# Turning three quarters of x and the query weight in the DMA, and moving the sums of Z, in a two-branch linear attention kernel

## The chip, the cores and the metric

The kernel runs on one core of one Trainium2 chip. The metric is the device time of one execution in microseconds; the kernel before takes 341.06 us (median of 3 runs, 340.96 to 342.13). A core has five engines that run side by side and wait for each other through semaphores: PE (TensorE, matmuls and transposes by matmul), DVE (VectorE), ACT (ScalarE), POOL (GpSimd) and SP (SyncE, which here only issues DMAs). Each engine carries out its instructions in the order of the program.

## The reference

Two attention branches read the same x (2048 tokens of 640 numbers, 32 heads of 20) and are mixed by a gate. Branch A makes features from softmaxes over the 20 numbers of a head, in both signs, and is linear in the keys:

```python
x = A_x
g = _sigmoid((x * gate_w).sum(-1, keepdims=True))
a = _A_ref(x, A_wqkv, A_w_phi, A_wo)
b = _B_ref(x, B_wq, B_wk, B_wv, B_wo, B_beta)
return g * a + (1 - g) * b
...
phi_q = jnp.concatenate([_softmax(pq, axis=-1), _softmax(-pq, axis=-1)], axis=-1)
phi_k = jnp.concatenate([_softmax(pk, axis=-1), _softmax(-pk, axis=-1)], axis=-1)
kv = jnp.einsum('bhsf,bhsd->bhfd', phi_k, v)
z = jnp.einsum('bhsf->bhf', phi_k)
num = jnp.einsum('bhqf,bhfd->bhqd', phi_q, kv)
den = jnp.einsum('bhqf,bhf->bhq', phi_q, z)[..., None] + 1e-06
o = num / den
```

Here z is the sum of the key features over all 2048 tokens. Branch B is causal softmax attention in four segments of 512 tokens with a memory carried from segment to segment; the change doesn't touch it.

## The kernel before

The order of every engine's instructions is that of the program text (manual schedules). The work falls into stages.

**Loading and folding (lines 95 to 308).** SP issues the loads of half the key weight, of x in eight pieces of 256 tokens (`emit_xload`, line 99, tile x_nat, six buffers), of the gate vector and of the value weight WvA. The key weight is turned on PE (`emit_foldT`: five transposes into PSUM and one copy to WkT), and multiplied with w_phi (`emit_foldM`) into WkA. `emit_xT(sc)` turns 128 tokens of x: five PE transposes (xtp, line 190) and one ACT copy into xT (line 192). Chunks 0 to 3 are turned among the fold products.

**The key loop (lines 312 to 322), 16 chunks of 128 tokens.** In step sc PE first turns x for chunk sc+4; then `emit_a1(sc)` makes ten matmuls to pk and ten to pv (line 214). A chunk is not 128 consecutive tokens: chunk sc = 4g + r holds every fourth token, starting with r, of the 512 tokens of quarter g (xTk, line 206). ACT takes two exponentials (Ek, line 218) and copies pv to vA (line 220); DVE sums over the 20 numbers of a head (ksum, line 222) and inverts (krec, line 225); POOL multiplies (EkSn, line 226). `emit_zmove(sc)` issues two DMAs from SP (line 234), one for each sign: they fold EkSn's 128 token rows into 16 partitions of Z with 8 rows each. In steps 9 to 13 PE also turns one fifth of the query weight (wnat_q, loaded in step 2) into WkT; after the loop `emit_foldM` multiplies it to WqA (line 325).

**Sums over tokens (lines 378 to 387).** `emit_kv(j, sgn, scs)` sums key features times values over the chunks on PE (kv_ps, line 368), in two PSUM tiles, one for each sign; DVE takes each block out with a mask (kvn, line 373). Blocks 0 and 3 come first (chunks 0 to 13, then 14 and 15), then 1, 2 and 4. `emit_zadd(ts)` (line 239) adds rows t of Z to row 0, one DVE instruction for each of the 31 rows: rows 1 to 5 behind block 1, 6 to 13 behind block 2, 14 to 31 behind block 4. SP then issues the loads of branch B's weights and the two output weights (lines 396 and 401).

**Query features (lines 479 to 494).** Ten steps (qb, j) of `emit_pq`: ten matmuls (pq, line 265) and two ACT exponentials (Eq, line 270). After step (0, 4) DVE finishes the gate (`emit_gS`). After step (1, 0) come `emit_z` (five PE transposes of Z's row 0, zt), `emit_zz` (33 small DVE instructions, lines 249 to 252, and two products to kvd, line 254) and POOL memsets over Z (`open_stages`). After step (1, 3) PE makes the denominators of chunks 0 to 3 (`emit_den`, line 410, 48 small matmuls of kvd), and DVE and POOL turn them into factors (`den_chain`).

**The loop over the 16 query chunks (line 528) and branch B** follow. The loop opens with the numerators of chunk 0 (line 527, tiles num0 and num1) and the denominators of chunks 4 and 5, whose PSUM tiles take over the memory of the tiles before. The transposing DMAs that the kernel already has are here: lines 520 (128 x 1024 numbers) and 556 (128 x 640), from SBUF to SBUF.

Of the kernel before, what the change touches and what calls it, by code (L numbers as in the profile page):

```python
# [7 lines left out]
ACT = mybir.ActivationFunctionType  # L8
ALU = mybir.AluOpType
BF16 = mybir.dt.bfloat16  # L10
# [5 lines left out]
def kernel(  # L16
# [15 lines left out]
    nc = tc.nc  # L32
    P = 128
    S = 2048
# [22 lines left out]
    back = const.tile([P, 4, 4, 8, 4], BF16, name="back")  # L57
# [14 lines left out]
    wq_stack = ExitStack()  # L72
    wq_hold = wq_stack.enter_context(tc.tile_pool(name="wq_hold", bufs=1))
    x_stack = ExitStack()
    xload = x_stack.enter_context(tc.tile_pool(name="xload", bufs=6))
    aps_stack = ExitStack()
    aps = aps_stack.enter_context(tc.tile_pool(name="aps", bufs=4, space=bass.MemoryType.PSUM))

    wnat_k = wq_hold.tile([P, KC, D], BF16, name="wnat_k", tag="wnat")
# [7 lines left out]
    def wsrc(lo):  # L87
        return A_wqkv[:, lo:lo + D].rearrange("(c p) n -> p c n", p=P)
# [19 lines left out]
    nc.sync.dma_start(out=gw5, in_=gate_w.rearrange("(c p) -> c p", p=P))  # L108
    for bk in range(2):
        nc.sync.dma_start(out=WvA[:, :, bk, 0:320], in_=wsrc(2 * D)[:, :, bk * 320:(bk + 1) * 320])  # L110
    for n in range(4):
        emit_xload()
    nc.sync.dma_start(out=beta_b, in_=B_beta.partition_broadcast(P))

    nc.gpsimd.memset(ident_b, 0.0)
# [32 lines left out]
                                fill=val, base=-row, channel_multiplier=1)  # L148


    nc.gpsimd.memset(back, 0.0)
# [4 lines left out]
    for u in range(4):  # L156
        nc.gpsimd.tensor_copy(out=back[:, u, :, :, u], in_=r32.rearrange("p (b t) -> p b t", t=8))

    def emit_Wphi(j):
        h0, h1 = TH[j]  # L160
        nc.vector.tensor_tensor(out=Wphi[:, j, 0:h1 - h0, :],
# [4 lines left out]
    def w2tile(name):  # L166
        return aps.tile([P, 2, 512], F32, name=name, tag="w2")
# [19 lines left out]
    def emit_xT(sc):  # L187
        tp = aps.tile([P, KC, P], BF16, name="xtp", tag="w2")
        for c in range(KC):
            nc.tensor.transpose(out=tp[:, c, :], in_=x_nat[sc // 2][:, sc % 2, c * P:(c + 1) * P],  # L190
                                identity=ident_b)
        nc.scalar.copy(out=xT[:, :, sc * P:(sc + 1) * P], in_=tp)
# [4 lines left out]
    a1w = kv_stack.enter_context(tc.tile_pool(name="a1work", bufs=3, side="right"))  # L197
    kvpool = kv_stack.enter_context(tc.tile_pool(name="kvpool", bufs=1, side="right"))
    EkSn = kvpool.tile([P, NCH, 2, D], BF16, name="EkSn")
    vA = kvpool.tile([P, NCH, 2, 321], BF16, name="vA")  # L200
    zt = zpool.tile([P, KC, P], BF16, name="zt")
    zz = zpool.tile([P, KC, 2, 2], BF16, name="zz")
# [2 lines left out]

    xTk = xT.rearrange("p c (g m r) -> p c g r m", g=4, r=4)

    def emit_a1(sc):
        pk, pv = w2tile("pk"), w2tile("pv")
        for ps, W, n in ((pk, WkA, 320), (pv, WvA, 321)):  # L210
            for bk in range(2):
                for c in range(KC):
                    rhs = WvA[:, c, bk, :] if W is WvA else WkA[:, c, bk * 320:(bk + 1) * 320]
                    nc.tensor.matmul(ps[:, bk, 0:n], lhsT=xTk[:, c, sc // 4, sc % 4], rhs=rhs,  # L214
                                     start=(c == 0), stop=(c == KC - 1))
# [10 lines left out]
        nc.gpsimd.tensor_tensor(  # L226
            out=EkSn[:, sc].rearrange("p s (h f) -> p (s h) f", f=DH),
            in0=Ek.rearrange("p s (h f) -> p (s h) f", f=DH),
            in1=krec[:, :, None].to_broadcast([P, 2 * H, DH]), op=ALU.mult)

    def emit_zmove(sc):
        g, r = divmod(sc, 4)
        for sgn in range(2):
            nc.sync.dma_start(out=Z[64 * sgn + 16 * g:64 * sgn + 16 * g + 16, r:32:4],
                              in_=EkSn[:, sc, sgn, :])

    def emit_zadd(ts):
        for t in ts:
            nc.vector.tensor_tensor(out=Z[:, 0, :], in0=Z[:, 0, :], in1=Z[:, t, :], op=ALU.add)
# [5 lines left out]
        nc.vector.tensor_copy(out=zt, in_=zt_ps)  # L245

    def emit_zz():
        ztv = zt.rearrange("p j (s h w) -> p j s h w", s=2, h=2)
        nc.vector.tensor_copy(out=zz, in_=ztv[:, :, :, :, 0])
        for w in range(1, 32):  # L250
            nc.vector.tensor_tensor(out=zz, in0=zz, in1=ztv[:, :, :, :, w], op=ALU.add)  # L251
        nc.vector.tensor_tensor(out=zcol, in0=zz[:, :, :, 0], in1=zz[:, :, :, 1], op=ALU.add)
        for sgn in range(2):
            nc.vector.tensor_tensor(out=kvd[:, sgn, :, :, 0], in0=wmw,
                                    in1=zcol[:, :, sgn:sgn + 1].to_broadcast([P, KC, HW]), op=ALU.mult)

    HB = 1024
    Eqs = {}
    def emit_pq(qb, j):
        Eq = Eq0[:, j] if qb == 0 else a3e.tile([P, 2, HB], BF16, name="Eq")  # L260
        pq = w2tile("pq")
        for half in range(2):
            for c in range(KC):
                t0 = qb * HB + half * 512
                nc.tensor.matmul(pq[:, half, :], lhsT=WqA[:, c, j * P:(j + 1) * P],  # L265
                                 rhs=xT[:, c, t0:t0 + 512],
                                 start=(c == 0), stop=(c == KC - 1))
        pqf = pq.rearrange("p b n -> p (b n)")
        for sgn in range(2):
            nc.scalar.activation(out=Eq[:, sgn, :], in_=pqf, func=ACT.Exp, scale=1.0 - 2.0 * sgn)  # L270
        Eqs[qb, j] = Eq

    def emit_beta():
        eb = const.tile([P, H], F32, name="eb")
# [31 lines left out]
    nc.tensor.transpose(out=gw_ps, in_=gw5, identity=ident_b[0:KC, 0:KC])  # L306
    nc.vector.tensor_copy(out=WvA[:, :, :, 320:321],
                          in_=gw_ps[:, :, None, None].to_broadcast([P, KC, 2, 1]))
    for n in range(2):
        emit_xload()  # L310
    wnat_q = wq_hold.tile([P, KC, D], BF16, name="wnat_q", tag="wnat")
    for sc in range(NCH):
        if sc + 4 < NCH:
            emit_xT(sc + 4)
        emit_a1(sc)
        emit_zmove(sc)
        if sc == 2:
            nc.sync.dma_start(out=wnat_q, in_=wsrc(0))
        if sc == 7:
            omgh_b, CM = emit_beta()  # L320
        if 9 <= sc < 14:
            emit_foldT(wnat_q, WkT, sc - 9, nc.scalar.copy if sc % 2 else nc.vector.tensor_copy)
    x_stack.close()
    for n in range(KC):
        emit_foldM(WkT, WqA, n)
# [12 lines left out]
    def emit_gate():  # L338
        gt_ps = aps.tile([P, NCH], F32, name="gt_ps", tag="w2")
        for u in range(4):  # L340
            nc.tensor.matmul(gt_ps, lhsT=back[:, u].rearrange("p b t v -> p (b t v)"),
                             rhs=xg[:, u].rearrange("p g a -> p (g a)"), start=(u == 0), stop=(u == 3))
        nc.scalar.activation(out=eg, in_=gt_ps, func=ACT.Exp, scale=-1.0)

    def emit_gS():
# [8 lines left out]
    def emit_kv(j, sgn, scs):  # L354
# [16 lines left out]
        if scs[-1] == NCH - 1:  # L371
# [3 lines left out]
                in0=kv_tiles[sgn][:, bk, off:off + n].rearrange("p (h d) -> p h d", d=DH),  # L375
                in1=wmw[:, j, h0 - g0:h1 - g0, None].to_broadcast([P, h1 - h0, DH]), op=ALU.mult)

    for scs in (range(14), range(14, NCH)):
        for j in (0, 3):
            for sgn in range(2):  # L380
                emit_kv(j, sgn, scs)
    for j, ts in ((1, range(1, 6)), (2, range(6, 14)), (4, range(14, 32))):
        for sgn in range(2):
            emit_kv(j, sgn, range(NCH))
        if j == 1:
            emit_gate()
        emit_zadd(ts)
# [582 lines left out]
```

## Time and profile before

| | us |
|---|---|
| Median of the runs | 341.06 |
| Profiled execution, its own time | 340.92 |
| Its span, first to last instruction | 339.2 |
| PE busy | 317.5 |
| ACT busy | 259.6 |
| DVE busy | 224.8 |
| POOL busy | 209.2 |

The stages in the span: loading and folding to 12.4 us, the key loop to 60.6, fold of the query weight to 62.7, sums over tokens to 75.1, query features to 101.6, the query loop to about 142, branch B to the end. The granted TensorE clock is 0.995 on the mean. A chain line gives start, duration, engine and tile or line; a timeline line gives start, duration, engine, line, operation, tiles, shape, count and, in brackets, how long the engine had been idle and who released it.

### The profile page before, as it was taken

The numbers are of one execution on the slowest core, as the hardware profiler recorded it, in microseconds if no ns is written. First come the engines' busy times: TensorE is split into PE (matmuls) and PEld (weight loads), VectorE is DVE, ScalarE is ACT, GpSimd is POOL, SyncE is SP. The second block draws the span as 40 slices with busy tenths as digits, with TensorE's granted clock in tenths as the row PEclk, the third lists the DMA queues.
The fourth block names the chain that finished last, engine by engine and source line by source line (L and its number), as shares of the span: only waits on it lengthen the run. The fifth ranks groups of instructions, "written<-read, shape, count | busy, mean of one in ns | idle before, by whom it ended". The sixth has DMA issues, their size and how long they took to land.

```text
span 339.2 us, 9735 instructions
## 1 busy us (share of the span) xinstructions
PE 317.5 (94%) x4021; PEld 219.2 (65%) x4021; DVE 224.8 (66%) x448; ACT 259.6 (77%) x331; POOL 209.2 (62%) x301
## 2 busy tenths in 40 slices
PE   6899999989978999988999999999999999999994
PEld 6788888874436877745665556556666656665662
DVE  3466887479877889726877686767666665453452
ACT  4888887508845455689999999999889889889842
POOL 8177678500406878864766666767867777666540
PEclk9999999999979999999999999999999999999999
DMA  8839969896003688754633255363564663421222
GB/s 232 277 70 180 121 96 118 123 294 208 0 2 24 124 117 122 119 107 81 95 64 57 41 101 95 58 108 64 92 83 87 123 88 73 87 60 51 45 72 77
DMA packets 83381, 34.21 MB, mean 101 GB/s; under 512 B 69258, under 2 KB 83338, under 8 KB 83338
## 3 DMA queue, kind: packets, MB, share of 16 engines
q1 hardware_dynamic: 82906, 33.11, 52.5%
q8 instruction: 31, 0.51, 0.7%
q10 hardware_dynamic: 432, 0.49, 0.6%
q14 instruction: 12, 0.10, 0.1%
HBM read 9.21 MB, written 2.62 MB: 35 GB/s over the span
## 4 chain that ended last, share of the span: by engine, by line
PE 61%; ACT 17%; DVE 10%; DMA 6%; issue 4%; POOL 1%; SPq 0%; ACTq 0%; DVEq 0%
ACT PT L625 15%; PE st_ps L621 10%; PE proj L755 9%; PE nda L677 7%; PE pk L214 6%; PE pv L214 6%; PE proj L808 6%; PE pq L265 5%; PE proj L506 3%; DVE tt L454 3%; DMA x_nat<-in_A_x_dram 2%; PE num L410 2%; DVE zz L251 2%; DVE rr L432 2%; DMA Z<-EkSn 1%
## 5 line engine op out<-in xcount | busy, mean ns | idle before, releaser
L625 ACT ACTIVATE PT<-st_ps 128x1024 bf16<-128x1024 f32 x160 | 154.4, 1025 | 15.9 <-PE st_ps L621 13.2
L632 POOL TENSOR_SCALAR_AFFINE_SELECT PT<-PT 128x512 bf16<-128x512 bf16 (+1 forms) x130 | 86.9, 687 | 48.0 <-ACT PT L625 47.9
L226 POOL TENSOR_TENSOR EkSn<-Ek,krec 128x1280 bf16<-128x1280 bf16 x16 | 37.6, 2358 | 17.9 <-DVE krec L225 16.2
L677 PEld LDWEIGHTS <-PT 128*128 128x128 bf16 x1280 | 39.8, 96 | 11.6 <-issue 8.4
L677 PE MATMUL nda<-vB,PT 128*128 128x21 bf16 x1280 | 42.8, 173 | 1.2 <-DVE mtmp L720 0.8
L214 PEld LDWEIGHTS <-xTf 128*128 128x128 bf16 x320 | 35.3, 113 | 6.8
L808 PEld LDWEIGHTS <-xTf 128*128 128x128 bf16 x320 | 28.0, 97 | 17.3 <-issue 8.0
L814 DVE CAST Z<-proj 128x320 bf16<-128x320 f32 x48 | 22.8, 486 | 22.6 <-PE proj L808 22.1
L222 DVE TENSOR_REDUCE ksum<-Ek 128x64 f32<-128x1280 bf16 x16 | 23.6, 1478 | 12.7 <-ACT Ek L218 12.7
L270 ACT ACTIVATE Eq<-pq 128x1024 bf16<-128x1024 f32 x20 | 19.4, 1021 | 14.2 <-PE pq L265 14.2
L454 DVE TENSOR_TENSOR tt<-num,rr 128x640 f32<-128x640 f32 x32 | 25.2, 812 | 6.2 <-PE num L410 4.3
L621 PE MATMUL st_ps<-Z 32*128 32x512 bf16 (+3 forms) x256 | 24.9, 299 | 4.1 <-ACT PT L625 2.1
L545 POOL TENSOR_TENSOR oA<-tt 128x640 bf16<-128x640 f32 x16 | 24.6, 1543 | 5.1 <-DVE tt L454 4.4
L755 PE MATMUL proj<-WkA,oTA 128*128 128x320 bf16 x160 | 27.3, 299 | 0.0
L218 ACT ACTIVATE Ek<-pk 128x640 bf16<-128x640 f32 x32 | 20.8, 701 | 7.5 <-PE pk L214 5.0
L410 PEld LDWEIGHTS <-Eq 128*128 128x128 bf16 x384 | 20.3, 97 | 9.4 <-issue 6.7
L621 PE MATMUL st_ps<-Eq 32*128 32x384 bf16 (+3 forms) x256 | 24.8, 299 | 1.4 <-ACT PT L625 0.8
L717 POOL TENSOR_TENSOR oB<-td 128x320 bf16<-128x320 f32 x23 | 19.8, 861 | 8.9 <-DVE td L714 5.8
L214 PE MATMUL pv<-WvA,xTf 128*128 128x321 bf16 x160 | 24.6, 300 | 0.0
L214 PE MATMUL pk<-WkA,xTf 128*128 128x320 bf16 x160 | 24.3, 299 | 0.0
L265 PE MATMUL pq<-xTf,WqA 128*128 128x512 bf16 x100 | 23.1, 392 | 0.0
L755 PE MATMUL proj<-WvA,oT 128*128 128x320 bf16 x120 | 22.6, 300 | 0.0
(142 smaller groups left out, 544.4 us busy)
## 6 DMA issues: line engine op xcount, KB each, us to landing
Z<-EkSn SPq DMA_DIRECT2D x32, 160.0 KB, 4.9
x_nat<-in_A_x_dram SPq DMA_DIRECT2D x8, 320.0 KB, 6.5
out_dram<-orow SPq DMA_DIRECT2D x10, 160.0 KB, 1.9
WvA<-in_A_wqkv_dram SPq DMA_DIRECT2D x2, 400.0 KB, 6.5
wnat_q<-in_A_wqkv_dram SPq DMA_DIRECT2D x1, 800.0 KB
WkB<-in_B_wk_dram SPq DMA_DIRECT2D x1, 800.0 KB, 7.2
WqB<-in_B_wq_dram SPq DMA_DIRECT2D x1, 800.0 KB, 9.0
WvB<-in_B_wv_dram SPq DMA_DIRECT2D x1, 800.0 KB, 10.6
```

Source lines behind the costliest of these rows:

```text
L214: nc.tensor.matmul(ps[:, bk, 0:n], lhsT=xTk[:, c, sc // 4, sc % 4], rhs=rhs, start=(c == 0), stop=(c == KC - 1))
L226: nc.gpsimd.tensor_tensor(out=EkSn[:, sc].rearrange("p s (h f) -> p (s h) f", f=DH), in0=Ek.rearrange("p s (h f) -> p (s h) f", f=DH), in1 ...
L265: nc.tensor.matmul(pq[:, half, :], lhsT=WqA[:, c, j * P:(j + 1) * P], rhs=xT[:, c, t0:t0 + 512], start=(c == 0), stop=(c == KC - 1))
L410: nc.tensor.matmul(ps(bk, lo, hi), lhsT=Eqs[qb, j][:, sgn, qc * P:(qc + 1) * P], rhs=kvx[:, sgn, j, lo - h0:hi - h0, :].rearrange("p h e - ...
L454: nc.vector.tensor_tensor(out=tt[:, sgn].rearrange("p (b h) d -> p b h d", b=2), in0=ps, in1=csb, op=ALU.mult)
L545: nc.gpsimd.tensor_tensor(out=oA.rearrange("p (h d) -> p h d", d=DH), in0=tt[:, 0], in1=tt[:, 1], op=ALU.add)
L621: nc.tensor.matmul(ps[:, i - i0, o:o + L - c * P], lhsT=kT[32 * i:32 * i + 32, c * P:(c + 1) * P], rhs=qT[32 * i:32 * i + 32, c * P:L], st ...
L625: nc.scalar.activation(out=PT[:, i0:i0 + 2], in_=ps, func=ACT.Exp, scale=SCALE_B)
L632: nc.gpsimd.affine_select(out=v, in_=v, pattern=[[0, n_i], [1, P]], compare_op=ALU.is_ge, fill=0.0, base=0, channel_multiplier=-1)
L677: nc.tensor.matmul(nd[:, j, i], lhsT=block(st, c)[:, i, (j - c) * P:(j - c + 1) * P], rhs=vB[:, c, 4 * st.g + i, :], start=(c == 0), stop= ...
L755: nc.tensor.matmul(ps, lhsT=oT[:, k % KC], rhs=W[:, k % KC, hs], start=(k == 0), stop=(k == n - 1))
L808: nc.tensor.matmul(ps, lhsT=xT[:, k, sc * P:(sc + 1) * P], rhs=W[:, k, half * 320:(half + 1) * 320], start=(k == 0), stop=(k == KC - 1))
```

## The change

Four things change, in what the instructions do and where they stand.

1. Only the first quarter of x is still loaded as x_nat and turned on PE. The other three quarters go into xT by three transposing DMAs from HBM, 512 x 640 numbers each (`emit_xturn`): two are issued by SP behind the loads of WvA, the third behind the Z moves of step 1. The query weight goes into WkT by one transposing DMA, issued behind the Z moves of step 5.
2. The chunks of the last quarter hold runs of 8 consecutive tokens, 16 runs 32 tokens apart. ACT gathers them from xT into a tile xP with four copies in steps 8 to 11 (`emit_xrun`). The Z moves write partitions 4 apart, and the last quarter's chunk r fills rows 8r to 8r+7 of Z; `emit_zz` reads the columns in the matching order. The gate takes its last four columns with a second set of matrices, back_run.
3. The 31 additions of Z stand elsewhere: rows 1 to 3 behind step 14 of the key loop, 4 to 9 before blocks 0 and 3, 10 to 15 behind these, 16 to 21 behind block 1, 22 and 23 behind block 2, 24 to 31 behind block 4.
4. `emit_gS`, `emit_z`, `emit_zz` and `open_stages` stand before query step (0, 4), and the first denominators behind step (1, 2).

```diff
-    xload = x_stack.enter_context(tc.tile_pool(name="xload", bufs=6))
+    xload = x_stack.enter_context(tc.tile_pool(name="xload", bufs=2))
...
+    xP = wq_hold.tile([P, KC, S // 4], BF16, name="xP")
...
-    for n in range(4):
-        emit_xload()
+
+    def emit_xturn(g):
+        nc.sync.dma_start_transpose(out=xT[:, :, 512 * g:512 * g + 512], in_=x2[512 * g:512 * g + 512, :])
+
+    def emit_xrun(r):
+        nc.scalar.copy(out=xP[:, :, r * P:(r + 1) * P].rearrange("p c (s u) -> p c s u", u=8),
+                       in_=xT[:, :, 1536:2048].rearrange("p c (s r u) -> p c s r u", r=4, u=8)[:, :, :, r])
+
+    emit_xturn(1)
+    emit_xturn(2)
...
+    def key_tokens(c, sc):
+
+        g, r = divmod(sc, 4)
+        return xTk[:, c, g, r] if g < 3 else xP[:, c, r * P:(r + 1) * P]
...
-            nc.sync.dma_start(out=Z[64 * sgn + 16 * g:64 * sgn + 16 * g + 16, r:32:4],
+            nc.sync.dma_start(out=Z[64 * sgn + g:64 * sgn + 64:4, r:32:4] if g < 3 else
+                              Z[64 * sgn + g:64 * sgn + 64:4, 8 * r:8 * r + 8],
                               in_=EkSn[:, sc, sgn, :])
...
-    for n in range(2):
-        emit_xload()
-    wnat_q = wq_hold.tile([P, KC, D], BF16, name="wnat_q", tag="wnat")
     for sc in range(NCH):
-        if sc + 4 < NCH:
-            emit_xT(sc + 4)
         emit_a1(sc)
         emit_zmove(sc)
-        if sc == 2:
-            nc.sync.dma_start(out=wnat_q, in_=wsrc(0))
+        if sc == 1:
+            emit_xturn(3)
+        if 8 <= sc < 12:
+            emit_xrun(sc - 8)
         if sc == 7:
             omgh_b, CM = emit_beta()
-        if 9 <= sc < 14:
-            emit_foldT(wnat_q, WkT, sc - 9, nc.scalar.copy if sc % 2 else nc.vector.tensor_copy)
+        if sc == 5:
+            nc.sync.dma_start_transpose(out=WkT, in_=A_wqkv[:, 0:D])
+        if sc == 14:
+            emit_zadd(range(1, 4))
...
+    emit_zadd(range(4, 10))
     for scs in (range(14), range(14, NCH)):
         for j in (0, 3):
             for sgn in range(2):
                 emit_kv(j, sgn, scs)
-    for j, ts in ((1, range(1, 6)), (2, range(6, 14)), (4, range(14, 32))):
+    emit_zadd(range(10, 16))
+    for j, ts in ((1, range(16, 22)), (2, range(22, 24)), (4, range(24, 32))):
         for sgn in range(2):
             emit_kv(j, sgn, range(NCH))
...
         for j in range(KC):
-            emit_pq(qb, j)
             if (qb, j) == (0, KC - 1):
                 emit_gS()
-            if (qb, j) == (1, 0):
                 emit_z()
                 emit_zz()
                 open_stages()
-            if (qb, j) == (1, 3):
+            emit_pq(qb, j)
+            if (qb, j) == (1, 2):
```

More of the change, by code (lines that the diff above doesn't have):

```diff
@@ L56 @@
     bd01 = const.tile([P, 4], F32, name="bd01")
-    back = const.tile([P, 4, 4, 8, 4], BF16, name="back")
     EPS_HI = 1.0 / 2 ** 20 + 3.0 / 2 ** 26
@@ L74 @@
     x_stack = ExitStack()
-    xload = x_stack.enter_context(tc.tile_pool(name="xload", bufs=6))
+    xload = x_stack.enter_context(tc.tile_pool(name="xload", bufs=2))
     aps_stack = ExitStack()
     aps = aps_stack.enter_context(tc.tile_pool(name="aps", bufs=4, space=bass.MemoryType.PSUM))
-    wnat_k = wq_hold.tile([P, KC, D], BF16, name="wnat_k", tag="wnat")
+    wnat_k = wq_hold.tile([P, KC, D], BF16, name="wnat_k")
+    xP = wq_hold.tile([P, KC, S // 4], BF16, name="xP")
     Wc = wq_hold.tile([P, KC, DH], BF16, name="Wc")
@@ L148 @@
                                 fill=val, base=-row, channel_multiplier=1)
-    nc.gpsimd.memset(back, 0.0)
     r32 = const.tile([P, 32], BF16, name="r32")
@@ L155 @@
         nc.gpsimd.tensor_tensor(out=r32, in0=r32, in1=ident_b[:, 32 * n:32 * n + 32], op=ALU.add)
-    for u in range(4):
-        nc.gpsimd.tensor_copy(out=back[:, u, :, :, u], in_=r32.rearrange("p (b t) -> p b t", t=8))
     def emit_Wphi(j):
@@ L199 @@
     EkSn = kvpool.tile([P, NCH, 2, D], BF16, name="EkSn")
+    back = kvpool.tile([P, 4, 4, 8, 4], BF16, name="back")
+    back_run = kvpool.tile([P, 4, 4, 4, 8], BF16, name="back_run")
+    nc.gpsimd.memset(back, 0.0)
+    for u in range(4):
+        nc.gpsimd.tensor_copy(out=back[:, u, :, :, u], in_=r32.rearrange("p (b t) -> p b t", t=8))
+    nc.gpsimd.memset(back_run, 0.0)
+    for u in range(4):
+        nc.gpsimd.tensor_copy(out=back_run[:, u, :, u, :], in_=r32.rearrange("p (b t) -> p b t", t=8))
     vA = kvpool.tile([P, NCH, 2, 321], BF16, name="vA")
@@ L213, in emit_a1 @@
                     rhs = WvA[:, c, bk, :] if W is WvA else WkA[:, c, bk * 320:(bk + 1) * 320]
-                    nc.tensor.matmul(ps[:, bk, 0:n], lhsT=xTk[:, c, sc // 4, sc % 4], rhs=rhs,
+                    nc.tensor.matmul(ps[:, bk, 0:n], lhsT=key_tokens(c, sc), rhs=rhs,
                                      start=(c == 0), stop=(c == KC - 1))
@@ L247, in emit_zz @@
     def emit_zz():
-        ztv = zt.rearrange("p j (s h w) -> p j s h w", s=2, h=2)
-        nc.vector.tensor_copy(out=zz, in_=ztv[:, :, :, :, 0])
+        ztv = zt.rearrange("p j (s a h b) -> p j s h b a", s=2, h=2, b=2)
+        nc.vector.tensor_copy(out=zz, in_=ztv[:, :, :, :, 0, 0])
         for w in range(1, 32):
-            nc.vector.tensor_tensor(out=zz, in0=zz, in1=ztv[:, :, :, :, w], op=ALU.add)
+            nc.vector.tensor_tensor(out=zz, in0=zz, in1=ztv[:, :, :, :, w // 16, w % 16], op=ALU.add)
         nc.vector.tensor_tensor(out=zcol, in0=zz[:, :, :, 0], in1=zz[:, :, :, 1], op=ALU.add)
@@ L255, in emit_zz @@
                                     in1=zcol[:, :, sgn:sgn + 1].to_broadcast([P, KC, HW]), op=ALU.mult)
[L257 to L271, printed above, removed]
     def emit_beta():
@@ L340, in emit_gate @@
         for u in range(4):
-            nc.tensor.matmul(gt_ps, lhsT=back[:, u].rearrange("p b t v -> p (b t v)"),
-                             rhs=xg[:, u].rearrange("p g a -> p (g a)"), start=(u == 0), stop=(u == 3))
+            nc.tensor.matmul(gt_ps[:, 0:12], lhsT=back[:, u].rearrange("p b t v -> p (b t v)"),
+                             rhs=xg[:, u, 0:3].rearrange("p g a -> p (g a)"), start=(u == 0), stop=(u == 3))
+        for u in range(4):
+            nc.tensor.matmul(gt_ps[:, 12:16], lhsT=back_run[:, u].rearrange("p b v t -> p (b v t)"),
+                             rhs=xg[:, u, 3], start=(u == 0), stop=(u == 3))
         nc.scalar.activation(out=eg, in_=gt_ps, func=ACT.Exp, scale=-1.0)
@@ L376, in emit_kv, with emit_pq @@
                 in1=wmw[:, j, h0 - g0:h1 - g0, None].to_broadcast([P, h1 - h0, DH]), op=ALU.mult)
+    HB = 1024
+    Eqs = {}
+    def emit_pq(qb, j):
+        Eq = Eq0[:, j] if qb == 0 else a3e.tile([P, 2, HB], BF16, name="Eq")
+        pq = w2tile("pq")
+        for half in range(2):
+            for c in range(KC):
+                t0 = qb * HB + half * 512
+                nc.tensor.matmul(pq[:, half, :], lhsT=WqA[:, c, j * P:(j + 1) * P],
+                                 rhs=xT[:, c, t0:t0 + 512],
+                                 start=(c == 0), stop=(c == KC - 1))
+        pqf = pq.rearrange("p b n -> p (b n)")
+        for sgn in range(2):
+            nc.scalar.activation(out=Eq[:, sgn, :], in_=pqf, func=ACT.Exp, scale=1.0 - 2.0 * sgn)
+        Eqs[qb, j] = Eq
+    emit_zadd(range(4, 10))
     for scs in (range(14), range(14, NCH)):
```

## The prediction

> **What bounds the kernel now.** I read the chain of waits in order of time, then the timeline around each place where the chain changes engine, then the DMA landings. The chain first (start, length, engine and line):
>
> ```profile
> 12.15 0.45 PE xtp L190 x5
> 12.60 1.36 PE pk L214 x10
> 13.96 1.38 PE pv L214 x10
> 15.33 0.28 PE xtp L190 x5
> ...
> 63.10 2.37 POOL EkSn L226
> 65.48 0.55 SPq L234
> 66.08 4.98 DMA Z<-EkSn
> ...
> 73.01 2.14 PE kv_ps L368 x32
> 75.15 12.95 PE pq L265 x60
> ...
> 98.30 3.26 PE pq L265 x10
> ```
>
> PE carries the key loop: 1.36 + 1.38 + 0.28 for a chunk. Then the chain goes through the last EkSn, its Z move, DVE and back to PE for the query products. Between 75.15 + 12.95 and 98.30 it is on DVE (zt, zz, kvd). The timeline shows PE's waits in that part:
>
> ```profile
> 12.15 0.45 PE L190 MATMUL xtp<-ident_b,x_nat 128*128 128x128 bf16 x5 [0.87 <-DMA x_nat<-in_A_x_dram]
> ...
> 66.84 0.49 PE L368 MATMUL kv_ps<-vA,EkSn 128*128 128x140 bf16 x4 [0.27 <-DVE kvn L373]
> ...
> 73.01 2.14 PE L368 MATMUL kv_ps<-vA,EkSn 128*128 128x140 bf16 x32 [0.90 <-DVE kvn L373]
> 73.10 4.16 DVE L239 TENSOR_TENSOR Z<-Z 128x640 bf16<-128x640 bf16 x8
> ...
> 96.88 1.42 PE L410 MATMUL den<-kvd,Eq 128*128 128x24 bf16 x48 [2.03 <-DVE kvd L254]
> ...
> 103.57 0.75 PE L410 MATMUL den<-kvd,Eq 128*128 128x24 bf16 x24 [1.10 <-ACT Eq L270]
> ```
>
> Two things to see. PE waits for kvn before it writes another half of the same PSUM tile (at 73.01 block 4, in the other bank, waits for the kvn of block 2): so kvn, and any Z addition ahead of it on DVE, paces PE. And behind the 2.03 us gap the granted clock fell; in the row of one microsecond (busy time of PE, PEld, DVE, ACT, POOL, then clock, DMA share, GB/s) it is 0.50, and the ten matmuls at 98.30 took 3.26 us, where six such groups took 12.95 (2.16 each).
>
> ```profile
> 98.00:99.00 1.00, 1.00 (x15) 0.45 (x12) 0.56 (x1) 0.00 (x0) 0.00 (x0) 0.50 0.00 0
> ```
>
> **1. Start: -1.06.** PE no longer waits at 12.15 for the third piece of x. What is next is WkA's last block, cast at 11.21 for 0.82, so to 12.03; the first four products of pk run before it, the fifth and the other bank's five (0.136 each) end at 12.9, against 13.96. WvA is no later: its loads stand at the same places ahead of the turns.
>
> **2. Key loop: -4.48.** The starts of pk stand 3.01 apart with one transpose group, 3.29 with two, 2.73 in the last two steps with none. The excess over 2.73 sums to 9 x 0.28 + 0.56 + 0.55 + 3 x 0.28 = 4.48. Nothing else reaches 2.73 in a step: POOL 2.36 (EkSn), DVE 1.49 + 0.55, ACT 1.30 + 0.69, and with the four added copies (not in the trace; between the 0.70 of xtp's copy and the 0.74 of the 640-number ACT copy at L561; I take 0.74) 2.73, just covered; were they twice as long, ACT would lag 3 us over four steps, and the two PSUM tiles that pk and pv have each hide most of it. The loop so ends at 60.60 - 1.06 - 4.48 = 55.1. The added POOL work (back_run, copies of 0.69 and a memset of 0.53) ends near 11.2, before EkSn's first at 17.5, and costs nothing.
>
> This holds if the turns land in time. HBM turns do not occur in the trace; the nearest rows are these:
>
> ```profile
> oTA<-oA SPq DMA_TRANSPOSE x16, 2.6
> Z<-Z SPq DMA_TRANSPOSE x16, 3.3
> ...
> 110.00:111.00 1.00, 0.74 (x9) 0.66 (x9) 1.00 (x3) 1.00 (x2) 0.00 (x0) 1.00 1.82 267
> ```
>
> A turn of 160 KB (oA) lands after 2.6 us, and 267 GB/s were moved in a microsecond with nothing but turns in flight. x's turn is four of these, 640 KB: at least 2.5 us at 267 GB/s, at most 10.4 if four ran one after the other; I take 4.5, from the 120 GB/s at a DMA share of 0.82 of the stage 110 to 130, scaled to full share. SP's issue of one takes 1.21 now, so 1.2 to 4.8: the first two are issued by 14.6 at the latest, before the first Z move (near 19). Ahead of them in the queue are 2.3 MB (key weight 800 KB, x 640, WvA 800), moved by 9.5 us at the 246 GB/s of the first ten. The quarters land near 16 and 21, by the upper bound at 20 and 30; they are needed at pk(4), 22.3, and pk(8), 33.2. The third and the query weight's stand among Z moves; the last such move that matters is step 12's, near 52, and by then SP (1.2 us for two moves in 2.73) has caught up.
>
> **3. A new wait: Z additions inside the loop, +2.** DVE gets rows 1 to 3 behind step 14 and ahead of ksum(15). Row 0 takes data from step 12, so they wait for its move. pk(12) starts at 49.11 - 1.06 - 3.9 = 44.1; EkSn(12) ends 7.6 later (49.11 to 56.71 now), at 51.7; the second DMA is issued at 52.3; it lands 3.6 to 6.5 later:
>
> ```profile
> DMA to landing us min/median/max: 3.6/4.9/6.5
> ```
>
> DVE is free at 55.1 (krec(14) ends 5.5 after its pk), so it waits till 56.9 (I take 4.6, since the writes now spread over four times as wide a stretch of partitions), adds three rows at 0.52 each to 58.5, and only then begins ksum(15), which could have started at 55.3. ksum, krec and EkSn take 4.6 more: the last EkSn, call it E, ends at 63.1 (62.1 to 65.0), against 65.48 now. PE has folded (2.16) and done 56 products of kv (3.56) by 60.8, and then waits some 2.3 us, a gap that is not there now. Without the additions there, E would be 59.9 and PE would hardly wait.
>
> The gap at 96.88 halved the clock after 2.03 us of idleness; if that happens here too, products paced by DVE slow by about 0.4. The Trainium skill, TensorE: Matmul & The Clock Gate, section Why this matters for your kernels, allows gaps up to about 3 us. The row shows a fall after 2.03 us, so page and row differ; by the page the sum would be 0.2 better. I take 0.2, half of it.
>
> **4. Sums over tokens: DVE paces PE.** From E: xg and rows 4 to 9 (6 x 0.52) end at E+1.0; the kvn of blocks 0 and 3, with PE between, at E+2.1; PE makes block 1 to E+4.0 and the gate (eight small products for four, 0.2 more, in a wait); DVE adds rows 10 to 15 to E+5.2, kvn(1) to 5.8, rows 16 to 21 to 8.9, kvn(2) to 9.5. Block 2 starts at E+5.6, block 4, which waits for kvn(2), at E+9.2, and ends at E+11.4. Now it is E+9.7 (65.48 to 75.15). So the query products begin at 63.1 + 11.4 + 0.2 = 74.7, against 75.15: of the 5.5 us won, 0.45 are left. The eight additions behind block 4 end 4.5 us into the query products, needed at 8.6.
>
> **5. Query features: -2.6.** From the start Q of the products: four groups 8.63, zt 0.29, four groups 8.63, so PE reaches den0 at Q+17.55. kvd is ready 8.47 after zt (88.39 to 96.86 now), at Q+17.40: the 2.03 wait is hidden by four groups instead of three, but barely; each us by which zz is late costs one. den0 1.42, two groups 4.32 at full clock (1.1 less than now for one of them), so pq(1, 4) ends at Q+23.3 = 98.0, and den_chain lies under the two groups. Then den of chunks 4 and 5 waits for Eq(1, 4) as now and ends 2.75 later (101.56 to 104.31), if PSUM tiles fall as now; the order of the tiles has changed, and if num0 takes the last product's place, its 0.97 comes behind the wait too. Between 0 and 0.97 I take 0.5: 101.3, against 104.31.
>
> **Sum: -3.0** (-1.06 - 4.48 + 5.1 given back in parts 3 and 4, - 2.6). Span 339.2 to 336.2, execution 340.92 to 337.9. The runs' median stands 0.14 above that execution: **338.1**. What follows is only shifted; branch B's weights land by 84, needed past 100.
>
> **Rivals.** (a) DVE doesn't wait for the move of step 12: it lands by 55.1, and only the 1.56 us of additions delay ksum(15). Then E = 61.3, 1.8 earlier, and without the gap the clock stays: 336.1. For it: the moves' writes are spread. Against it: it needs a landing in 2.8 us, and none took under 3.6. 10 in 100. (b) The gain is eaten: a landing of 6.5 (E = 65.0, +1.9), the late num0 (+0.5) and the slow clock (+0.2), which together leave 0.4: 340.7, no change. For it: moves stood at 5.3 to 5.7 near the loop's end. 22. (c) Slower: the turns from HBM are slow. With b us for each 128 x 128 block (20 in a turn, one after the other from 9.5) the third ends at 9.5 + 60b, and is needed, through ACT's copies, near 43; the loop slips by 60b - 33, so the gain of 3.0 is gone at b = 0.6 and at b = 0.75 the slip of 12 makes 350. Against it: five blocks land in 2.6 us, 0.52 each with all latency; for it: the source is HBM in pieces of 256 bytes, which no row shows. 14. The Trainium skill, VectorE: DVE Perf Modes, section The three transpose paths, gives 1.31 us for one block through the DMA and 0.39 on PE; blocks taken one after the other, that would be 26 us for a turn, and by an estimate a slip of 45 us. The trace disagrees (five blocks in 2.6 us); I give it 2 of the 14.
>
> **Chances.** Forecast 54, (a) 10, (b) 22, (c) 14. 0.5% (1.7 us) is about what a measurement of this kernel tells from no change: faster is below 339.35. The forecast's own range (E from 62.1 to 64.3, num0, clock) is 336.4 to 339.6, a little of which is within 0.5%: faster 0.60, same 0.23, slower 0.17. The range from 335.0 to 342.8 holds all of these but most of (c).
>
> **What would show it.** pk 2.73 apart from 12 us, no PE wait for xTf at steps 4, 8, 12; DVE idle near 55 to 57 until the move of step 12, PE idle 2 us before the kv products of chunks 14 and 15; PE waiting for kvn twice, about 1 us, in blocks 2 and 4; no wait at den0 and a clock of 1.0 there. The forecast is wrong if the turns hold pk back, or if PE needn't wait for kvn.

## The result, and the profile after

The kernel after takes **360.5 us** (median of 4 runs, 360.42 to 361.89), the kernel before 341.08 beside it: a ratio of 1.057, with a 95% interval of 1.054 to 1.061. It is slower by 19.4 us, where 338.1, a faster kernel, had been forecast. The profiled execution has a span (first to last instruction) of 358.7, against 339.2 before.

The loss lies at the start of the key loop, at a place where the prediction had put nothing. First the timeline of PE in the kernel after (start, length, line, operation, tiles, count; in brackets the idle time before and what ended it):

```profile
13.49 0.33 PE L231 MATMUL pk<-WkA,xTf 128*128 128x320 bf16 x1 [0.85 <-ACT xTf L196]
17.16 2.56 PE L231 MATMUL pk<-WkA,xTf 128*128 128x320 bf16 x9 [3.35 <-DMA xTf<-in_A_x_dram]
...
36.40 2.59 PE L231 MATMUL pk<-WkA,xTf 128*128 128x320 bf16 x9 [10.80 <-DMA xTf<-in_A_x_dram]
...
40.76 1.52 PE L231 MATMUL pk<-WkA,xTf 128*128 128x320 bf16 x10
```

The count is what to read. The ten products of pk(0) are split into 1 and 9: the first one runs, the second waits 3.35 us for a turn of x. Yet chunk 0 holds tokens of quarter 0 alone, which PE turned and ACT copied; no turn writes what it reads. (A turn is one of the transposing DMAs.) Chunk 2, also of quarter 0, is split in the same way (its first product ran at 25.30) and its other nine wait 10.80 us. Then it is over: from 40.76 on the loop has no such wait.

The chain of waits over the same stretch (start, length, what) says what each wait hung on:

```profile
5.47 5.76 SPq L113
...
11.28 5.75 DMA xTf<-in_A_x_dram
...
30.64 0.60 SPq L251
...
31.33 5.02 DMA xTf<-in_A_x_dram
```

pk(0) waits for the second turn, landed at 17.03. Chunk 2 waits for the third, and that one stands in SP's queue behind the Z moves of step 1 (line 251), which need EkSn(1): so it could not even be issued before 31.33. The PE gap of 10.80 us holds a trip through ACT, DVE, POOL, SP and the DMA. While PE stood still the granted clock went down too, in the row of one microsecond (PE, PEld, DVE, ACT, POOL, then clock, DMA share, GB/s):

```profile
34.00:35.00 1.00, 0.00 (x0) 0.00 (x0) 0.00 (x0) 0.00 (x0) 0.00 (x0) 0.50 1.27 290
```

So the nine products behind each gap took 2.56 and 2.59 us instead of 1.23, which is nine tenths of the 1.36 to 1.37 that ten products take in the chain at full clock.

Next the timeline of the sums, which answers to the lines around 66.84 and 73.01 before:

```profile
76.25 2.16 PE L184 MATMUL fold_ps<-Wphi,WkT 128*128 128x240 bf16 x30
...
77.39 2.59 DVE L257 TENSOR_TENSOR Z<-Z 128x640 bf16<-128x640 bf16 x3 [1.50 <-DMA Z<-EkSn]
...
82.02 5.14 DVE L257 TENSOR_TENSOR Z<-Z 128x640 bf16<-128x640 bf16 x6
...
84.77 0.53 PE L372 MATMUL kv_ps<-vA,EkSn 128*128 128x140 bf16 x3 [2.72 <-POOL EkSn L243]
...
87.43 0.63 PE L372 MATMUL kv_ps<-vA,EkSn 128*128 128x140 bf16 x4 [2.13 <-DVE kvn L377]
...
95.40 2.14 PE L372 MATMUL kv_ps<-vA,EkSn 128*128 128x140 bf16 x32 [1.09 <-DVE kvn L377]
```

DVE's wait of 1.50 for a Z move inside the loop and PE's wait of 2.72 for the last EkSn are there, as forecast (1.8 and 2.3). Not forecast is that three additions took 2.59 and six took 5.14 us: 3 x 0.52 and 6 x 0.52 are 1.56 and 3.1. The chain has one addition of 1.55 us in the three and one of 2.54 in the six, all others at 0.49 to 0.50. The group of Z's additions by itself (minimum, median, maximum in ns):

```profile
L257 DVE TENSOR_TENSOR Z<-Z x31: 478/492/2523, 77.4 to 101.5; 128x640 bf16<-128x640 bf16 x31
```

The first denominators (96.88 before) no longer wait, and the next wait is for Eq, the exponentials of the query products:

```profile
114.92 1.35 PE L433 MATMUL den<-kvd,Eq 128*128 128x24 bf16 x48
...
122.63 0.96 PE L433 MATMUL num<-kvn,Eq 128*128 128x240 bf16 x12 [2.03 <-ACT Eq L396]
```

The prediction's own points, beside what the profiled execution shows:

| us from the span's start | predicted | after | difference added here |
|---|---|---|---|
| key loop ends, fold starts | 55.1 | 76.25 | +21.15 |
| E, the last EkSn ends | 63.1 | 84.71 | +0.46 |
| Q, the query products start | 74.7 | 97.54 | +1.2 |
| denominators of chunks 4 and 5 end | 101.3 | 124.2 | +0.0 |
| span | 336.2 | 358.7 | -0.4 |

Q is read in the chain of waits, as the prediction read it (the timeline has 97.38). All but about 1.4 of the 22.5 us between forecast and profile arose before 76.25. Of the 21.15, the two waits are 14.15; the half clock behind them is 4.9 (pk(0), pv(0) and pk(1) took 1.33, 1.32 and 0.34 longer than at full clock, pk(2) and pv(2) 1.36 and 0.57); and the remaining 2.1 are a late start: PE began pk(0) at 13.49, so without any wait it would have ended at 15.04 (ten products in one piece take 1.55 there, as e3 below shows), against 12.9.

### The profile page after: what moved, and what is told of

Same layout as the page of the kernel before. It is cut to its first block, busy times and chain, and to the rows that moved or that the text cites. A ratio compares the mean times of both kernels' runs of the same rounds, so it can differ in the third digit from the quotient of the medians.

```text
span 358.7 us, 9573 instructions
## 1 busy us (share of the span) xinstructions
PE 319.6 (89%) x3937; PEld 217.3 (61%) x3940; DVE 226.2 (63%) x446; ACT 253.0 (71%) x320; POOL 211.2 (59%) x306
## 4 chain that ended last, share of the span: by engine, by line
PE 54%; ACT 18%; DVE 12%; DMA 5%; issue 5%; POOL 3%; SPq 2%; ACTq 0%; DVEq 0%; POOLq 0%
ACT PT L647 15%; PE st_ps L643 9%; PE proj L777 9%; PE nda L699 7%; PE pq L391 6%; PE proj L830 5%; PE pk L231 4%; PE proj L528 3%; POOL EkSn L243 3%; DMA xTf<-in_A_x_dram 3%; DVE Z L257 3%; PE pv L231 3%; PE num L433 2%; DVE tt L477 2%; PE kv_ps L372 2%
## 5 line engine op out<-in xcount | busy, mean ns | idle before, releaser
L231 PEld LDWEIGHTS <-xTf 128*128 128x128 bf16 x240 | 28.2, 118 | 24.4 <-DMA xTf<-in_A_x_dram 11.1
L830 PEld LDWEIGHTS <-xTf 128*128 128x128 bf16 x320 | 28.0, 97 | 17.1 <-issue 7.6
L231 PE MATMUL pk<-WkA,xTf 128*128 128x320 bf16 x120 | 21.4, 329 | 15.0 <-DMA xTf<-in_A_x_dram 14.1
L396 ACT ACTIVATE Eq<-pq 128x1024 bf16<-128x1024 f32 x20 | 19.4, 1021 | 11.1 <-DMA WvA<-in_B_wo_dram 7.6
L433 PEld LDWEIGHTS <-Eq 128*128 128x128 bf16 x384 | 20.3, 96 | 7.9 <-issue 4.9
L391 PE MATMUL pq<-xTf,WqA 128*128 128x512 bf16 x97 | 21.9, 379 | 0.2
L433 PE MATMUL num<-kvn,Eq 128*128 128x240 bf16 (+2 forms) x192 | 17.8, 229 | 3.8 <-ACT Eq L396 2.0
```

The lines of the kernel that those rows point to most:

```text
L231: nc.tensor.matmul(ps[:, bk, 0:n], lhsT=key_tokens(c, sc), rhs=rhs, start=(c == 0), stop=(c == KC - 1))
L433: nc.tensor.matmul(ps(bk, lo, hi), lhsT=Eqs[qb, j][:, sgn, qc * P:(qc + 1) * P], rhs=kvx[:, sgn, j, lo - h0:hi - h0, :].rearrange("p h e - ...
L830: nc.tensor.matmul(ps, lhsT=xT[:, k, sc * P:(sc + 1) * P], rhs=W[:, k, half * 320:(half + 1) * 320], start=(k == 0), stop=(k == KC - 1))
```

## The experiments

The theory, "cover": a turn writes five column blocks of 512 tokens, 2048 elements apart in xT, and it is treated as one write from the first of them to the last. Within that stretch lie the blocks of the quarters that it doesn't write, and whoever loads one of these waits for it. Column block 0 of quarter 0 lies ahead of every such stretch, blocks 1 to 4 lie inside. The trace agrees: the weight load of pk(0) at column block 0 waits for the semaphore of ACT's copy alone, that at block 1 for those of both turns ahead of it in the program. That is where the count splits into 1 and 9. The rival: the turns are slow, or PE stands still for some other reason while they run.

**e1: the third turn early.** It is issued right behind the second; all else as after.

```diff
     emit_xturn(2)
+    emit_xturn(3)
...
-        if sc == 1:
-            emit_xturn(3)
```

> Theory (cover): the first product of chunk 0 that reads x's second column block waits for every turn issued ahead of it in the program, and those of chunk 2 for the third turn, though both chunks hold tokens of the first quarter only, because a turn's write is taken as one stretch from its first to its last column block. With all three turns issued ahead of the loop, pk of chunk 0 waits for the third one, to about 21 to 22 us instead of 17, and chunk 2 doesn't wait at all: 10.8 us of wait and some 1.8 of half clock go, 4 to 5 come: about 353 (351 to 355). Rival (place): chunk 2's wait is only that the third turn was issued late behind the Z moves, and each chunk needs no more than its quarter: chunk 0 starts at 17 as before and the time is 347 to 349.

Measured: 352.54 us (median of 2 runs), ratio 1.033 (1.029 to 1.038), span 350.7: inside the theory's 351 to 355, outside the rival's 347 to 349. Chunk 2 waits no longer. Chunk 0 now waits for three turns instead of two, the third issued at 15.40, as the chain of waits of this kernel has it:

```profile
15.40 5.57 DMA xTf<-in_A_x_dram
...
21.11 2.56 PE pk L232 x9
```

So the wait goes with the place of a turn in the program, and not with the data that a chunk reads. No turn was made faster, and 8 us came back, of which 1.0 is that pk(0) began earlier (12.46 instead of 13.49); that the third turn's place caused this too is not shown.

**e2: a turn for each column block.** Fifteen DMAs instead of three, each with one unbroken stretch for its output.

```diff
-        nc.sync.dma_start_transpose(out=xT[:, :, 512 * g:512 * g + 512], in_=x2[512 * g:512 * g + 512, :])
+        for c in range(KC):
+            nc.sync.dma_start_transpose(out=xT[:, c, 512 * g:512 * g + 512],
+                                        in_=x2[512 * g:512 * g + 512, c * P:(c + 1) * P])
```

> Theory (cover): each turn is five DMAs of 512 x 128, one for each column block, so that each writes one unbroken stretch of xT. No chunk waits for a quarter that it doesn't read: pk of chunk 0 starts near 13, all steps are 2.73, the loop ends near 56: 338 to 341 us. More issues on SP (15 for 3, some 1.2 us each) may cost up to 1 of it. Rival (slow turns): the DMA brings the quarters too late whatever waits are placed; pk waits at chunks 4 and 8 and the time stays above 346.

Measured: 342.13 us, ratio 1.003 (1.000 to 1.006), span 341.0. No PE wait for a turn is left, and the place of the third turn behind step 1 is unchanged:

```profile
12.02 1.55 PE L233 MATMUL pk<-WkA,xTf 128*128 128x320 bf16 x10 [0.85 <-ACT xTf L198]
```

The same bytes are turned at the same places of the program: what differs is the form of the outputs, and with it the number of DMAs. The waits are gone as the theory has it, but the time is above its 338 to 341; e3 shows why.

**e3: xT laid out by quarters.** The three DMAs stay whole; each quarter's five blocks lie together, so that a turn's output is one unbroken stretch of 5 x 512. The readers' views follow.

```diff
-    xT = xTf[:, 0:KC * S].rearrange("p (c t) -> p c t", c=KC)
+    xTg = [xTf[:, r * 512:(r + KC) * 512].rearrange("p (c t) -> p c t", c=KC) for r in (0, 6, 11, 16)]
...
-        nc.sync.dma_start_transpose(out=xT[:, :, 512 * g:512 * g + 512], in_=x2[512 * g:512 * g + 512, :])
+        nc.sync.dma_start_transpose(out=xTg[g], in_=x2[512 * g:512 * g + 512, :])
...
-                                 rhs=xT[:, c, t0:t0 + 512],
+                                 rhs=xTg[t0 // 512][:, c, :],
```

> Theory (cover): xT is laid out by quarters, so that each turn's write is one unbroken stretch; three turns as in the change. No wait for turns at chunks 0 to 3; loop ends near 56; den0 doesn't wait; 337 to 340 us. Rival (slow turns): waits of several us at chunks 4 and 8, above 345. Rival (something else in the change is slow too): no wait for turns, but above 341.

Measured: 341.95 us, ratio 1.002 (1.000 to 1.004), span 340.0. That is above the theory's 337 to 340: the waits are gone, and the rival that something else in the change is slow too holds as well. The timeline of PE shows the ten products of pk(0) in one piece:

```profile
12.22 1.55 PE L231 MATMUL pk<-WkA,xTf 128*128 128x320 bf16 x10 [0.85 <-ACT xTf L196]
```

The fold starts at 55.92, where 55.1 was predicted: with the output in one stretch the key loop is as forecast. In this trace the first weight load that waits for the first turn is that of chunk 4, and for the second turn that of chunk 8, the chunks that read them. So cover is shown from two sides (e2 and e3). By the medians after and e3 differ by 18.5 us; in the profiles the fold starts 20.3 earlier in e3, of which 19.1 are the waits and the half clock behind them, and 1.3 the late start of pk(0). But the loop's gain of 4.7 us (60.59 to 55.92) still ends in no gain at all: E is 64.38, Q 77.41 (74.99 before), and the span 340.0 instead of the 336.2 predicted. The timeline between shows where:

```profile
57.09 2.56 DVE L257 TENSOR_TENSOR Z<-Z 128x640 bf16<-128x640 bf16 x3 [1.53 <-DMA Z<-EkSn]
...
61.69 5.14 DVE L257 TENSOR_TENSOR Z<-Z 128x640 bf16<-128x640 bf16 x6
61.84 2.54 POOL L243 TENSOR_TENSOR EkSn<-Ek,krec 128x1280 bf16<-128x1280 bf16 x1 [3.60 <-DVE xg L335]
...
67.09 0.62 PE L372 MATMUL kv_ps<-vA,EkSn 128*128 128x140 bf16 x4 [2.30 <-DVE kvn L377]
...
67.88 3.89 PE L372 MATMUL kv_ps<-vA,EkSn 128*128 128x140 bf16 x32 [0.16 <-DVE kvn L377]
```

One of the six additions runs beside POOL's EkSn and takes as long as it (in the chain 62.20 to 64.74; EkSn 61.84 to 64.38). The kvn that PE needs is queued behind all six, PE waits 2.30, and then makes 32 products in 3.89 us instead of 2.11; the granted clock is 0.50 in each microsecond from 67 to 73.

**e4: no additions in the loop.** From e3; rows 1 to 3 join rows 4 to 9 behind the loop. Theory: their wait only moves, within 0.7 us; rival: their cost in the loop is real.

```diff
-        if sc == 14:
-            emit_zadd(range(1, 4))
...
-    emit_zadd(range(4, 10))
+    emit_zadd(range(1, 10))
```

> On the layout by quarters, the Z additions of rows 1 to 3 stand behind the loop instead of inside it. Theory (DVE paces the sums): the last EkSn ends 1.5 to 2 us earlier, but DVE then carries three more additions (1.56 us) ahead of the first kvn, so the query products start at the same time: within 0.7 us of the layout by quarters. Rival (the last EkSn sets the end of the stage): 1.5 to 2.5 us faster than it.

Measured: 339.62 us, ratio 0.996 (0.994 to 0.999): 2.3 below e3, so the theory's size missed and the rival's held. (The profiled execution, the fastest of the ten, has a span of 336.5.) Without DVE's wait of 1.53 and the slowed additions ahead of ksum(15), the last EkSn, which starts at 58.20, ends at 60.75 instead of 64.38. A part comes back: nine additions now stand ahead of the first kvn, and PE waits longer for it:

```profile
58.05 6.73 DVE L257 TENSOR_TENSOR Z<-Z 128x640 bf16<-128x640 bf16 x9
...
58.20 2.55 POOL L243 TENSOR_TENSOR EkSn<-Ek,krec 128x1280 bf16<-128x1280 bf16 x1 [0.19 <-DMA Z<-EkSn]
...
65.05 0.49 PE L370 MATMUL kv_ps<-vA,EkSn 128*128 128x140 bf16 x4 [3.38 <-DVE kvn L375]
```

**e5: additions only where DVE has time.** From e4: three additions ahead of blocks 0 and 3, three behind these, four and three more behind blocks 1 and 2, eighteen behind block 4; and, since Z is then complete later, Z's turn and its sums again before query step (1, 0) and the first denominators behind (1, 3).

```diff
-    emit_zadd(range(1, 10))
+    emit_zadd(range(1, 4))
...
-    emit_zadd(range(10, 16))
-    for j, ts in ((1, range(16, 22)), (2, range(22, 24)), (4, range(24, 32))):
+    emit_zadd(range(4, 7))
+    for j, ts in ((1, range(7, 11)), (2, range(11, 14)), (4, range(14, 32))):
...
+            if (qb, j) == (1, 0):
                 emit_z()
...
-            if (qb, j) == (1, 2):
+            if (qb, j) == (1, 3):
```

> Layout by quarters; Z additions so placed that few lie ahead of a kvn: rows 1 to 3 behind the loop, 4 to 6 behind blocks 0 and 3, 7 to 10 behind block 1, 11 to 13 behind block 2, the other 18 behind block 4; Z is turned before step (1, 0), and the first denominators come behind (1, 3). Theory (DVE's additions pace PE between the last EkSn and the query products): query products start near 70 to 71 instead of 75.1 (additions out of the loop) and 77.4 (layout by quarters), den0 hardly waits: 333 to 335.5 us. Rival (that stage is held by something else, such as the clock or the Z moves): no more than 1 us faster than the kernel with the additions out of the loop, 338.5 or above.

Measured: **332.23 us** (332.12 to 332.44), ratio 0.975 (0.972 to 0.978), span 330.4. It beats both kernels and lies below the theory's 333 to 335.5. In the timeline of PE the waits for kvn have shrunk to 0.27 and 0.18 us, the query products start at 69.19 instead of 75.06, and the denominators, at 88.89, still do not wait:

```profile
61.83 0.49 PE L370 MATMUL kv_ps<-vA,EkSn 128*128 128x140 bf16 x4 [0.27 <-DVE kvn L375]
...
64.65 4.70 PE L370 MATMUL kv_ps<-vA,EkSn 128*128 128x80 bf16 x96
69.19 10.96 PE L389 MATMUL pq<-xTf,WqA 128*128 128x512 bf16 x50
```

The count x96 in the second line holds block 2's 64 products and block 4's 32 in one run without a wait: DVE no longer paces PE. That additions placed ahead of kvn hold up PE is so shown. With the long waits the half clock is gone too: block 1's 32 products took 2.11 us, against 3.70 in e4. The run changes the additions' places and those of Z's sums together, so it doesn't say what each is worth.

**e6: without the fourth part.** From e3; `emit_gS`, `emit_z`, `emit_zz`, `open_stages` and the first denominators stand where they stood before.

```diff
+            emit_pq(qb, j)
             if (qb, j) == (0, KC - 1):
                 emit_gS()
+            if (qb, j) == (1, 0):
                 emit_z()
...
-            emit_pq(qb, j)
-            if (qb, j) == (1, 2):
+            if (qb, j) == (1, 3):
```

> Layout by quarters with the change's fourth part undone: Z turned behind step (1, 0), the first denominators behind (1, 3). Theory: the wait of 2.0 us for kvd and the half clock behind it (1.1) come back, the late num0 (1.0) goes: 1.8 to 3 us slower than the layout by quarters. Rival (the moved denominators bring nothing, their chain only waits elsewhere): within 0.7 us of it.

Measured: 341.32 us, ratio 1.003 (1.000 to 1.005): 0.6 below e3 instead of 1.8 to 3 above it. So the theory missed, and the rival, no more than 0.7 either way, holds. The timeline shows the wait back (but not its half clock: the ten products behind it took 2.32 us, and less of a wait for Eq followed):

```profile
98.40 1.34 PE L433 MATMUL den<-kvd,Eq 128*128 128x24 bf16 x48 [1.63 <-DVE kvd L272]
```

From Q to the end of chunk 4's and 5's denominators it takes 27.8 us (76.90 to 104.7), against 26.8 in e3 (77.41 to 104.2). So in the two profiles part 4 is worth some 1 us of these stretches, not the 2.6 predicted; in the medians no gain of it shows, and what takes it back is open.

**e7: the fourth part alone**, put into the kernel before (the same lines moved, the additions left where they were).

> The kernel before with the fourth part of the change alone: Z turned before step (0, 4), the first denominators behind (1, 2). Theory: the Z additions end at 87.0 and four groups of query products at 83.8, so PE waits 3.3 us at zt in place of 2.0 at den0, and its clock halves there: 0.5 to 2.5 us slower than before. Rival (the order of the denominators alone carries a gain): 1.5 to 3 us faster.

Measured: 340.88 us, ratio 1.000 (0.998 to 1.003). The wait of 2.03 at the denominators is gone, and another has come, since Z's additions are not done when PE turns Z:

```profile
86.85 0.45 PE L244 MATMUL zt_ps<-ident_b,Z 128*128 128x128 bf16 x5 [3.32 <-DVE Z L239]
87.14 10.48 PE L265 MATMUL pq<-xTf,WqA 128*128 128x512 bf16 x40
```

The forecast of this wait (3.3 us) was exact, while the loss expected of it was not there: behind the wait 40 products took 10.48 us instead of 8.80, and the later wait for Eq, 1.10 before, is gone. Neither the theory (0.5 to 2.5 slower) nor the rival (1.5 to 3 faster) holds: by itself part 4 is no change. Whether it gains once Z's additions come early enough is not shown, since e6 against e3 shows no gain in the medians either.

**e8: the query weight's turn alone**, put into the kernel before: one transposing DMA for WkT in step 5, no PE turns and copies in steps 9 to 13.

```diff
-        if sc == 2:
-            nc.sync.dma_start(out=wnat_q, in_=wsrc(0))
+        if sc == 5:
+            nc.sync.dma_start_transpose(out=WkT, in_=A_wqkv[:, 0:D])
...
-        if 9 <= sc < 14:
-            emit_foldT(wnat_q, WkT, sc - 9, nc.scalar.copy if sc % 2 else nc.vector.tensor_copy)
```

> The kernel before with the turn of the query weight alone done by one transposing DMA, behind the Z moves of step 5; x is turned on PE as before. Theory: five groups of PE transposes go, 5 x 0.28 = 1.4 us off the loop, no new wait (its tile is not read until after the loop): 339.0 to 340.2. Rival (a transposing DMA from HBM holds up the moves or the x pieces behind it): 341 or above.

Measured: 338.38 us, ratio 0.993 (0.990 to 0.996): 2.6 faster, more than the 339.0 to 340.2 expected. The fold starts at 59.06 instead of 60.59, which is 1.53 of it (five times 0.28 were 1.4). In the profiled execution another 1.07 is the clock behind the denominators' wait:

```profile
95.85 1.34 PE L407 MATMUL den<-kvd,Eq 128*128 128x24 bf16 x48 [2.04 <-DVE kvd L254]
97.06 2.32 PE L265 MATMUL pq<-xTf,WqA 128*128 128x512 bf16 x10
```

The wait is as long as before (2.04 against 2.03), yet the ten products take 2.32 us in the timeline, against 3.39 in the timeline of before. How much of the median's 2.6 this is, the single profile doesn't show.

## Why the prediction was wrong, point by point

- **The step that failed** is in part 2. "The quarters land near 16 and 21, [...] they are needed at pk(4), 22.3, and pk(8), 33.2." Their landing was no problem: they were in place at 14.8 and 17.03, earlier than forecast. Their need was wrong. It was taken from which chunk reads which tokens; but two turns were needed at pk(0)'s second column block, before 14, and the third at pk(2)'s, because the waits follow the stretch that a write spans. e1 moved the wait with the third turn, e2 and e3 took it away by the form of the output alone. It cost 14.15 us of waits and 4.9 of half clock. The prediction's own signs of turns that hold pk back looked at steps 4, 8 and 12; the waits were at steps 0 and 2.
- **"The third and the query weight's stand among Z moves"** was costed at nothing with step 12's move in view. But pk(2) waited for the third turn, and that stands behind moves that need EkSn(1): 10.80 of the 14.15 are this place in the queue. e1, where it was issued ahead, is 8 us faster, 7 of them by this.
- **Rival (c)**, slow turns, had the sign right and the mechanism wrong. The three turns of 640 KB, twenty 128 x 128 blocks each, landed 9.3, 5.75 and 5.0 us behind the start of their issue; the first, issued while loads ahead of it were still on their way, is the slowest in e1 and e3 too (10.5 and 10.2). That is at most 0.52 us for each block; the point from which (c) decides was 0.6. The Trainium skill, VectorE: DVE Perf Modes, section The three transpose paths, gives 1.31 us for one block; twenty blocks one after the other would be 26 us, by an estimate. The trace disagrees: these turns took 5.0 to 10.5. The prediction's 4.5 us for a turn was too short, and its upper bound of 10.4 just reached; SP's issue, put at 1.2 to 4.8, took 2.93 to 5.76, with no harm since nothing that is needed soon stood behind it at the start.
- **Part 1, -1.06:** too large. In e3 pk(0) ends at 13.76, not 12.9: what is next behind the third piece of x is ACT's copy of the quarter's last turned tokens (its chain has this copy end at 12.17, right ahead of pk(0)), not WkA's cast. The change is -0.2 there. In the profile of after pk(0) started another 1.3 late (13.49 against 12.22). There PE waits for a piece of the key weight till 5.50 instead of 5.05; where the rest comes from is open.
- **Part 2's turns themselves, -4.48:** right. From the end of pk(0) to the fold it is 42.16 us in e3 and 46.64 before, which is 4.48. The starts of pk stand 2.73 apart in after from chunk 3 on (40.76, 43.49), and the four xP copies took 0.73 to 0.75, as put (0.74), and held nobody.
- **Part 3, +2:** right in size (E is 8.46 behind the fold in after and e3, 8.0 predicted), but by luck, since two errors stood against each other. The moves landed in 2.7 us, not 4.6; but EkSn(12) was later, since POOL is still behind from the work of step 7 (in e3 it starts EkSn(8) after a pause of 3.05 and makes seven without one). In e3 EkSn(12) ends at 53.62, where 51.7 was forecast, and its second move lands at 57.01, where 56.9 was forecast. And three additions took 2.56, not 1.56. The heading's +2 is not what the part adds up to, which is 3.2 (63.1 against 59.9); e3 against e4 has 3.6 (64.38 against 60.75). Rival (a) had the landing right, 2.8 us, and not the rest: DVE waited all the same, because the move was issued later.
- **Part 4, Q = E + 11.6:** 12.8 in after, 13.2 in e3, in the chain. The mechanism (DVE paces PE, two waits for kvn) was right, though the first wait, 2.13, stood ahead of block 3's last products and not in block 2; the size missed, since "rows 4 to 9 (6 x 0.52)" took 5.14 beside EkSn and the gap slowed the clock more than the 0.2 allowed. The Trainium skill, SBUF — State Buffer, section Who interferes with whom, states that a DVE instruction with two SBUF inputs and a GpSimd instruction that reads SBUF exclude each other, and the second to come waits for the whole of the first. The traces agree: in e3 an addition that started at 62.20, behind the start of EkSn at 61.84, took 2.52 instead of 0.49 and ended 0.34 us after it. The prediction put additions beside EkSn twice and did not price it.
- **Part 5, -2.6:** the end of these products came where forecast, at Q + 26.6; no wait at the denominators, full clock, num0 behind the wait for Eq (2.03). But as a saving it was too large. Against a kernel with the same sums and the old places (e6) it is about 1 us in this stretch of the profiles and nothing in the medians, and part of the 2.6 is the half clock of before, which e6 and e8 don't have in the same place.
- **"What follows is only shifted":** right. From the end of those denominators to the end of the span it is 234.5, against 234.9 before.

Without the failed step the forecast would still have been 3.9 us too low (e3, 341.95): rival (b), the gain eaten, is what e3 shows in its outcome. Its mechanism was another (a landing of 6.5 us, where the moves took 2.7): 0.8 arose ahead of the fold, 0.5 with the additions in the loop, 1.6 from E to Q, and the rest mostly in slower products after the wait for Eq (the first five at 104.08 took 1.49 us, against 0.84 in e4). e4 and e5 show the same for the additions from the other side.

## What to carry to other kernels

In these kernels a consumer waits for a transfer by what the transfer's output spans, not by what it writes: before you replace small transfers by one large strided one, look at which instructions load from between its pieces, and give it an output in one unbroken stretch, by the layout or by several transfers. An in-order engine that feeds a faster one should do the work that is due first; what is due later goes behind it, even if the engine then looks idle for a moment (e4 to e5: 7.4 us with the same number of instructions on every engine, though Z's sums moved too). A gain ahead of such a queue can be worth nothing until the queue is put right (e3: 4.7 us at the fold, none at the end).

## What the runs showed of the hardware that was not expected

- A DVE addition of 128 x 640 bf16 takes 0.49 us, and 2.52 when it starts just behind POOL's multiplication of 128 x 1280, itself only little longer (2.36 to 2.54). Where it starts in the middle of one (77.39 in after, the multiplication from 76.21 to 78.58), it takes 1.54. Both times it ends about 0.35 us after the multiplication.
- The clock behind a PE gap of 2 us is not settled by its length. The products behind a gap of 2.03 ran at half clock in the profile of before (3.26 us for ten), those behind 2.04 in e8 did not. Behind num0's wait of 2.03, five products took 1.49 in e3 and 0.84 in e4. The 25 runs of before beside e1 to e4 agree: four, with a mean clock of 1.0, took 339.3 to 339.7, the others, with 0.988 to 0.995, 340.3 to 342.9. What decides is open.
- The Z moves, still sixteen partitions each but four apart instead of adjacent, landed in 2.7 us on the median; before it was 4.9, and in e8, where they are unchanged, 4.8:

```profile
Z<-EkSn SPq DMA_DIRECT2D x32, 160.0 KB, 2.7
```

This is the row of after among the transfers (count, size, median us from issue to landing). Whether the spread over partitions alone did it was not tried.
